# Another order of all engines' work in a fused windowed attention and highway layer

## The chip, the cores and the metric

The kernel runs on one core of a Trainium2 chip. The metric is the time of one execution on the device in microseconds (us), lower is better. Runs of the same kernel are compared by their median.

## The reference

Eight batches, eight heads, 576 positions, 64 values per head. Attention looks back over a window of 128 positions and has a bias that falls with the distance (slope by head). Its result, 4608 rows of 512 values, goes through a highway layer.

```python
scores = scale * q @ k.T                                # per batch and head
scores = where((rel >= 0) & (rel < 128), scores - slope[h] * rel, -1e9)
attn = softmax(scores)
x = (attn @ v)  -> rows of 512 (8 heads x 64)           # 4608 x 512
H = maximum(x @ w_h, 0)
T = 1 / (1 + exp(-(x @ w_t + b_t)))
out = T * H + (1 - T) * x
```

## The kernel before

The output is worked on in 36 blocks of 128 rows. A batch has four full blocks (0 to 3) and half a block, and the two halves of two neighbouring batches make one block 4, which carries the number of the odd batch. Keys are taken in five chunks of 128 for each batch (the fifth, with u = 4, is done with the fourth chunk's scores).

Nothing is scheduled by the compiler. The string `ORDER` holds some 650 words; a loop at the end goes through them, and each word issues one small piece of work. Each engine carries out its own instructions in the order of the words, and waits with semaphores where data or a buffer isn't ready. So the order of the words is the order of every queue: TensorE (PE), VectorE (DVE), ScalarE (ACT), GpSimd (POOL), and SyncE (SP), which only starts transfers. A word is a letter and its indices (batch, then block or chunk).

| word | what it issues | engine, line |
|---|---|---|
| `q b` (and `Q` at the start for halves of batch 0) | loads q and then k of a batch, turned to bf16 on the way | GpSimd's queue, L117 (L120) |
| `V b u`, `v b u` | loads a chunk of v, f32 | SyncE's queue; ScalarE's queue (L126) |
| `L i` | loads w_h or w_t | GpSimd's queue, L134 |
| `h` | one tiny write that keeps the load of V02 from starting early | VectorE, L139 |
| `T b w h` | transposes q (w=0) or k (w=1) of four heads | VectorE, L208 |
| `C b u`, `c b u` | casts a chunk of v to bf16 | GpSimd; ScalarE (L130) |
| `S b u` | scores of a chunk with its mask, into the one tile `sc` | TensorE, L229 and L246 |
| `E b u` | exp of `sc` | ScalarE, L260 |
| `P b t` | probabilities times v for a block, into the one tile `av` | TensorE, L289 |
| `N b t` | reciprocal of the sums and x | VectorE, L299 and L300 |
| `U b t` | transposes x | TensorE, L307 |
| `X b t`, `x b t` | copies the transposed x out | ScalarE; VectorE (L312) |
| `B b t` then `Z b t` | bias into the one tile `z`, then x @ w_t | ScalarE, L317, then TensorE, L332 |
| `z b t` | the same with the bias by a matmul | TensorE, L321 and L332 |
| `Y b t` | tanh of `z` | ScalarE, L338 |
| `H b t` | x @ w_h into the one tile `h` | TensorE, L344 |
| `R b t` | relu(h) - x | VectorE, L349 |
| `o b t`, `O b t` | tanh to gate | GpSimd; VectorE (L353) |
| `G b t`, `g b t` | times gate | GpSimd; VectorE (L357) |
| `A b t`, `a b t` | plus x, gives the output tile `ot` | GpSimd; VectorE (L361) |
| `D b t` | stores the block | SyncE's queue, L368 (L372 for block 4) |
| `M b` | clears the half-filled chunk of a v buffer | GpSimd, L204 |
| `i`, `J`, `F`, `f`, `k` | constants, masks and the bias | several |

A few buffers tie the words together: q and k have three loaded sets (batch b and b + 3 share one) and two transposed sets, v has three loaded and four cast sets, exp has four tiles and one more, `x` ten, and `tt`, `uu` and `ot` six each. `sc`, `av`, `z` and `h` have one.

Of the kernel before, what the change touches and what calls it, by code (L numbers as in the profile page):

```python
# [11 lines left out]


ORDER = """
i2 J V00 Q000 V01 i0 Q010 i1 Q001 Q011 q1 c00 i4 c01 M2 F L1 v03 L0 T000 T010 M1 q2 T001 f h
T011 k V02 V10 i5 V04 S00 E00  S01 P00 E01 N00 T101 U00 S02 X00 P01 E02 z00 N01 T111 U01 S03 x01
V14 c02 T100 Y00 V11 P02 E03 o00 H00 T110 z01 R00 N02 H01 Y01 c03 g00 o01 U02 a00 S10 X02 R01
P03 E10 G01 z02 N03 H02 A01 Y02 B03 U03 O02 R02 S11 X03 V12 C10 T210 G02 P10 E11 Z03 V23 N10 A02
H03 V21 Y03 U10 C11 R03 S12 X10 O03 V13 C12 B10 T211 P11 E12 G03 H10 V20 N11 Z10 A03 T201 V22
U11 Y10 q3 S13 x11 R10 D01 c13 P12 E13 O10 z11 C23 N12 D00 C14 V30 g10 U12 T200 H11 A10 X12 D02  # L20
Y11 D03 P13 R11 c04 C21 D10 S20 c22 N13 o11 B12 H12 g11 c20 A11 E20 U13 Z12 x13 R12 P14 H13 Y12
N14 B13 o12 S21 R13 q4 g12 U14 Z13 x14 a12 P20 Y13 H14 D12 N20 E21 D11 z14 O13 T300 G13 U20 X20
S22 R14 A13 Y14 T311 P21 E22 z20 D13 N21 V34 H20 O14 Y20 T301 U21 o20 S23 X21 T310 P22 E23 z21
N22 V24 C30 g14 U22 V31 R20 A14 S30 X22 T411 Y21 P23 E30 G20 z22 N23 A20 H21 T410 Y22 V32 U23
o21 R21 S31 X23 V33 B23 g21 P30 E31 H22 N30 V40 C31 Z23 a21 R22 U30 V41 C32 Y23 S32 x30 q5 B30
O22 P31 g22 V44 E32 O23 Z30 N31 A22 D14 H23 T401 V42 Y30 C40 U31 D21 S33 X31 R23 D22 B31 T400
V43 G23 P32 c34 H30 E33 N32 A23 Z31 o30 U32 c33 S40 x32 Y31 R30 P33 B32 g30 H31 E40 N33 A30 Z32
O31 R31 U33 c24 G31 S41 x33 Y32 P34 E41 A31 z33 N34 q6 T501 H32 Y33 D20 D23 B34 U34 T510 V54 S42
o32 X34 V50 o33 P40 E42 R32 Z34 C41 V51 N40 G32 H33 T511 Y34 U40 A32 S43 X40 R33 B40 P41 T500
E43 G33 H34 N41 Z40 A33 c42 U41 Y40 o34 S50 x41 R34 o40 P42 E50 g34 H40 N42 A34 z41 R40 c43 g40  # L30
U42 Y41 A40 S51 x42 V52 T610 P43 E51 C54 z42 N43 D32 C50 o41 T611 H41 Y42 V53 B43 U43 o42 T601
S52 X43 C44 D33 D31 P50 C51 E52 R41 Z43 D30 q7 N50 D34 H42 g41 Y43 T600 U50 S53 X50 o43 R42 C53
P51 E53 A41 z50 N51 g42 C52 D41 U51 Y50 H43 V62 x51 B51 a42 o50 D40 P52 V60 R43 Z51 g43 N52 A43
S60 Y51 U52 H50 X52 E60 P53 R50 z52 N53 H51 g50 Y52 O51 A50 B53 U53 R51 S61 x53 G51 T701 H52 E61
V61 P54 A51 V63 R52 Z53 O52 c62 N54 V71 C60 S62 Y53 T700 B54 o53 U54 H53 X54 D42 C61 g52 E62 P60
A52 R53 Z54 D51 N60 H54 V64 G53 Y54 D52 T711 U60 D43 o54 S63 X60 D50 R54 c63 A53 V72 P61 T710
B60 V73 H60 E63 G54 N61 Z60 A54 R60 U61 Y60 S70 x61 V70 O60 P62 g60 E70 A60 z61 V74 N62 C72 U62
D54 H61 X62 Y61 P63 R61 B62 o61 S71 N63 c64 C70 Z62 E71 g61 A61 U63 H62 x63 c71 D61 P70 Y62 S72
D53 N70 D60 B63 o62 U70 E72 Z63 x70 R62 P71 G62 H63 Y63 N71 B70 S73 o63 R63 c73 A62 g63 U71 Z70
x71 a63 C74 P72 Y70 H70 N72 B71 o70 E73 Z71 R70 U72 G70 H71 x72 Y71 P74 A70 R71 z72 N74 o71 D70  # L40
D63 U74 g71 H72 X74 a71 Y72 P73 D71 R72 o72 z74 D62 N73 G72 Y74 U73 H74 x73 o74 z73 A72 R74 g74
H73 Y73 a74 o73 D74 R73 D72 g73 a73 D73
"""


# [384 lines left out]
```

## Time and profile before

| what | value |
|---|---|
| time, median of 3 runs | 155.78 us (155.69 to 158.38) |
| the profiled execution's own time | 155.89 us |
| span of the profiled execution | 154.1 us, mean granted TensorE clock 0.995 |
| busy: TensorE, VectorE, ScalarE, GpSimd | 128.7, 121.3, 111.4, 93.0 us |
| moved by transfers | 29.76 MB, mean 193 GB/s |

The span goes from the first to the last instruction, and the time is a little longer. The profile's slices cut the span into 40 equal parts and show the busy share of each engine in tenths. The chain of work that ended last is followed back from the last instruction, at each step to what released it. A matmul's own duration overlaps that of the next, so the chain's pieces, and not the durations, add up. Line numbers are those of the code above.

### The profile page before, as it was taken

What the parts mean: (1) busy time and instruction counts of PE and PEld (TensorE: products, weight loads), DVE (VectorE), ACT (ScalarE), POOL (GpSimd) and SP (SyncE); (2) the same over time, 40 slices, a digit from 0 to 9 for tenths busy, and PEclk for the clock granted to TensorE, in tenths of its full rate; (3) what the DMA queues carried; (4) which work ended last, traced back from release to release, by engine and by line L of the source; (5) the groups of instructions that cost most, each with busy time, mean ns of one, the idle gap of its engine ahead of it and who ended that gap; (6) DMA issues with size and microseconds to landing.
All of it is one profiled execution on the core that took longest, in us unless ns stands there. A gap on an engine that the chain in (4) does not pass through costs nothing.

```text
span 154.1 us, 6258 instructions
## 1 busy us (share of the span) xinstructions
PE 128.7 (83%) x2754; PEld 73.0 (47%) x2754; DVE 121.3 (79%) x234; ACT 111.4 (72%) x127; POOL 93.0 (60%) x117
## 2 busy tenths in 40 slices
PE   0005489999999999999999996999999999999940
PEld 0001256455655565456665654554555656555510
DVE  5795158979997997799779975999699966796790
ACT  2222675899898698699999987685779989964410
POOL 7940001279985544865679987584297966577640
PEclk9999999999999999999999999999999999999997
DMA  4999999999999999999998999379993891500715
GB/s 107 197 206 207 202 201 209 212 174 207 273 156 200 311 242 271 202 200 188 213 284 194 207 235 327 120 116 192 303 239 120 260 218 41 208 5 3 269 37 167
DMA packets 48222, 29.76 MB, mean 193 GB/s; under 512 B 38466, under 2 KB 39490, under 8 KB 48196
## 3 DMA queue, kind: packets, MB, share of 16 engines
q1 hardware_dynamic: 41712, 18.62, 48.5%
q0 software_dynamic: 5440, 10.49, 38.4%
q10 hardware_dynamic: 1044, 0.27, 1.0%
q8 instruction: 21, 0.34, 0.9%
q14 instruction: 5, 0.04, 0.1%
HBM read 30.41 MB, written 9.44 MB: 259 GB/s over the span
## 4 chain that ended last, share of the span: by engine, by line
PE 47%; DVE 27%; DMA 8%; POOL 5%; issue 5%; ACT 4%; POOLq 0%; DVEq 0%
PE h L344 11%; PE z L332 11%; PE av L289 8%; DMA ld<-in_k_dram 8%; DVE tr L208 7%; PE sc L229 7%; DVE x L300 5%; DVE uu L349 4%; PE av L307 4%; PE sc L246 4%; DVE ot L361 3%; DVE uu L357 2%; ACT pr L260 2%; POOL ot L361 1%; POOL uu L357 1%
## 5 line engine op out<-in xcount | busy, mean ns | idle before, releaser
L260 ACT ACTIVATE pr<-sc 128x2048 bf16<-128x2048 f32 x28 | 52.6, 1877 | 7.6 <-PE sc L246 7.5
L361 POOL TENSOR_TENSOR ot<-uu,x 128x512 f32<-128x512 bf16 x28 | 32.3, 1155 | 13.9 <-DVE uu L357 13.0
L208 DVE STREAM_TRANSPOSE tr<-ld 128x576 uint32<-128x576 uint32 x32 | 38.9, 1242 | 1.7 <-DMA ld<-in_k_dram 1.7
L332 PE MATMUL z<-wT,xt 128*128 128x512 bf16 x144 | 37.8, 386 | 0.0
L344 PE MATMUL h<-wH,xt 128*128 128x512 bf16 x144 | 37.0, 379 | 0.1
L353 POOL TENSOR_SCALAR tt<-tt 128x512 f16<-128x512 f16 x25 | 15.6, 628 | 30.7 <-ACT tt L338 30.7
L338 ACT ACTIVATE tt<-z 128x512 f16<-128x512 f32 x36 | 21.5, 597 | 10.7 <-PE z L332 10.7
L349 DVE SCALAR_TENSOR_TENSOR uu<-h,x 128x512 bf16<-128x512 f32 x36 | 24.5, 682 | 4.2 <-PE h L344 4.2
L300 DVE TENSOR_TENSOR x<-av,rd 128x512 bf16<-128x512 f32 x36 | 24.9, 691 | 1.4
L289 PE MATMUL av<-va,pr 128*128 128x65 bf16 (+1 forms) x480 | 22.2, 197 | 0.4 <-DVE xt L312 0.3
L229 PE MATMUL sc<-tr,tr 32*64 32x192 bf16 (+2 forms) x1152 | 20.2, 253 | 2.8 <-ACT pr L260 2.0
L229 PEld LDWEIGHTS <-tr 32*64 32x64 bf16 x1152 | 13.4, 108 | 18.7 <-issue 15.5
L357 POOL TENSOR_TENSOR uu<-uu,tt 128x512 bf16<-128x512 bf16 x15 | 17.3, 1156 | 7.9 <-DVE uu L349 6.1
L289 PEld LDWEIGHTS <-pr 128*128 128x128 bf16 (+1 forms) x480 | 18.6, 101 | 6.8 <-issue 2.3
L332 PEld LDWEIGHTS <-xt 128*128 128x128 bf16 x144 | 13.5, 99 | 13.4 <-issue 1.0
L344 PEld LDWEIGHTS <-xt 128*128 128x128 bf16 x144 | 12.8, 98 | 12.2 <-issue 0.6
L307 PE MATMUL av<-ident,x 128*128 128x128 bf16 x144 | 14.5, 225 | 2.2 <-DVE x L300 2.0
L299 DVE RECIPROCAL rd<-av 128x8 f32<-128x8 f32 x36 | 7.0, 193 | 11.9 <-PE av L289 11.6
L307 PEld LDWEIGHTS <-x 128*128 128x128 bf16 x144 | 10.2, 100 | 12.5 <-DVE x L300 7.2
L312 ACT COPY xt<-av 128x512 bf16<-128x512 bf16 x19 | 11.1, 585 | 5.6 <-PE av L307 5.3
L130 POOL CAST va<-vs 128x512 bf16<-128x512 f32 x22 | 13.7, 632 | 1.5 <-DMA vs<-in_v_dram 1.5
L130 ACT CAST va<-vs 128x512 bf16<-128x512 f32 x18 | 11.0, 618 | 4.7 <-DMA vs<-in_v_dram 4.6
(47 smaller groups left out, 109.4 us busy)
## 6 DMA issues: line engine op xcount, KB each, us to landing
out_dram<-ot SPq DMA_DIRECT2D x32, 256.0 KB, 4.3
vs<-in_v_dram SPq DMA_DIRECT2D x31, 256.0 KB, 5.6
ld<-in_q_dram POOLq DMA_DIRECT2D x7, 576.0 KB, 8.3
ld<-in_k_dram POOLq DMA_DIRECT2D x7, 576.0 KB, 11.9
vs<-in_v_dram SPq DMA_DIRECT2D x8, 128.0 KB, 5.4
out_dram<-ot SPq DMA_DIRECT2D x8, 128.0 KB, 2.9
ld<-in_q_dram POOLq DMA_DIRECT2D x2, 288.0 KB, 6.9
ld<-in_k_dram POOLq DMA_DIRECT2D x2, 288.0 KB, 7.4
```

Source lines behind the costliest of these rows:

```text
L130: (eng.copy if eng is nc.scalar else eng.tensor_copy)(out=VA[b % 4][:, u, :, 0:D], in_=VS[b % 3][:, u])
L208: nc.vector.transpose(out=t[:, 0:S, :].rearrange("p s e -> p (s e)").bitcast(U32).rearrange("p (s t) -> p t s", t=NT), in_=ld[:, h].bitcas ...
L229: nc.tensor.matmul(out=SC[64 * g : 64 * g + 64, j, 256 * h + col : 256 * h + col + n], lhsT=TR[b % 2, 1, h][rows, key : key + 64, e], rhs= ...
L260: nc.scalar.activation(out=p[:].rearrange("p j h n -> p j (h n)"), in_=SC[:], func=ACTF.Exp, scale=scale)
L289: nc.tensor.matmul(out=av[o : o + m, h, 65 * j : 65 * j + 65], lhsT=PT[bb, pt][:, j, h, off : off + m], rhs=VA[bb % 4][:, u, 4 * h + j, :] ...
L300: nc.vector.tensor_tensor(out=x[:].rearrange("p (h j d) -> p h j d", h=2, j=NJ), in0=av[:, :, :, 0:D], in1=rd[:].to_broadcast([P, 2, NJ, D ...
L307: nc.tensor.transpose(out=AV[blk][:, c // 2, 272 + 64 * (c % 2) :][:, 0:64].bitcast(BF16), in_=X[blk][:, c * P : (c + 1) * P], identity=id ...
L332: nc.tensor.matmul(out=pz[:], lhsT=xt[:, c * P : (c + 1) * P], rhs=wT[:, c, :], start=False, stop=c == NC - 1, skip_group_check=True)
L344: nc.tensor.matmul(out=pa[:], lhsT=xt[:, c * P : (c + 1) * P], rhs=wH[:, c, :], start=c == 0, stop=c == NC - 1)
L349: nc.vector.scalar_tensor_tensor(out=uu[:], in0=PA.pop(blk)[:], scalar=0.0, in1=X[blk][:], op0=ALU.max, op1=ALU.subtract)
L357: eng.tensor_tensor(out=UU[blk][:], in0=UU[blk][:], in1=TT.pop(blk)[:], op=ALU.mult)
L361: eng.tensor_tensor(out=ot[:], in0=UU.pop(blk)[:], in1=X.pop(blk)[:], op=ALU.add)
```

## The change

Only the string `ORDER` is replaced. The new order comes from a search over orders, in which transfers were taken to last longer and to land later, and TensorE's instructions to run at a lower rate. No function is changed. The word counts that differ are those where a word has two forms on two engines:

| | B + Z | z | X | x | C | c | O | o | G | g | A | a | V | v |
|---|---|---|---|---|---|---|---|---|---|---|---|---|---|---|
| before | 19 | 17 | 19 | 17 | 22 | 18 | 11 | 25 | 15 | 21 | 28 | 8 | 39 | 1 |
| after | 13 | 23 | 20 | 16 | 20 | 20 | 15 | 21 | 10 | 26 | 27 | 9 | 37 | 3 |

The first lines, a stretch in the middle and the end of both orders:

```diff
-i2 J V00 Q000 V01 i0 Q010 i1 Q001 Q011 q1 c00 i4 c01 M2 F L1 v03 L0 T000 T010 M1 q2 T001 f h
-T011 k V02 V10 i5 V04 S00 E00  S01 P00 E01 N00 T101 U00 S02 X00 P01 E02 z00 N01 T111 U01 S03 x01
-V14 c02 T100 Y00 V11 P02 E03 o00 H00 T110 z01 R00 N02 H01 Y01 c03 g00 o01 U02 a00 S10 X02 R01
-P03 E10 G01 z02 N03 H02 A01 Y02 B03 U03 O02 R02 S11 X03 V12 C10 T210 G02 P10 E11 Z03 V23 N10 A02
...
-N14 B13 o12 S21 R13 q4 g12 U14 Z13 x14 a12 P20 Y13 H14 D12 N20 E21 D11 z14 O13 T300 G13 U20 X20
-S22 R14 A13 Y14 T311 P21 E22 z20 D13 N21 V34 H20 O14 Y20 T301 U21 o20 S23 X21 T310 P22 E23 z21
-N22 V24 C30 g14 U22 V31 R20 A14 S30 X22 T411 Y21 P23 E30 G20 z22 N23 A20 H21 T410 Y22 V32 U23
...
-D63 U74 g71 H72 X74 a71 Y72 P73 D71 R72 o72 z74 D62 N73 G72 Y74 U73 H74 x73 o74 z73 A72 R74 g74
-H73 Y73 a74 o73 D74 R73 D72 g73 a73 D73
+i2 J V00 Q000 V01 V10 i0 Q010 i1 Q001 Q011 M1 q1 i4 c00 V14 L1 L0 T000 T010 T001 c01 V12 h F v02
+f v03 T011 k S00 E00 S01 P00 E01 N00 i5 T100 U00 S02 X00 T110  P01 V11 c10 E02 z00 N01 U01 Y00
+S03 x01 T111 z01 T101 V13 c14 C02 E03 q2 P02 H00 N02 o00 S10 R00 V20 c03 U02 Y01 H01 x02 E10 O01
+V22 g00 P03 R01 A00 z02 g01 N03 A01 H02 Y02 c11 U03 C12 S11 x03 R02 P10 E11 O02 z03 N10 G02 U10
+A02 X10 S12 Y03 H03 v04 o03 E12 P11 R03 z10 N11 V21 C13 H10 T210 M2 q3 U11 R10 S13 X11 V30 Y10
...
+R11 U13 q4 S20 X13 O11 g11 Y12 P14 a11 E20 z13 N14 U14 Y13 x14 S21 O12 P20 E21 H12 N20 z14 R12
...
+P22 R14 V32 Y20 N22 S30 B21 H20 T410 E30 D00 C23 U22 Z21 T400 D01 C33 X22 S31 T411 V31 o20 Y21
+P23 o13 E31 z22 D02 N23 D03 D11 g13 U23 c30 A12 g14 V24 S32 x23 Y22 D10 R20 P30 E32 V34 A13 z23
...
+o22 S33 X31 V43 R22 C34 c24 P32 o23 g22 E33 a22 Z31 V42 q5 N32 H23 O30 Y31 q6 U32 S40 x32 D12
+c41 O31 R23 P33 E40 H30 N33 D13 V50 R30 U33 S41 X33 c40 P34 c43 H31 N34 E41 z32 R31 g30 U34 Y32
+H32 x34 g23 P40 R32 z33 N40 S42 Y33 U40 z34 X40 T510 P41 Y34 H33 E42 N41 o34 z40 T511 D20 V44
...
+N60 Z54 R52 U60 g52 Y54 S62 T700 X60 H53 E62 D41 C61 O54 T710 V74 A51 P61 V63 z60 N61 A52 R53
+S63 Y60 D50 C62 T701 D42 U61 G53 H54 D52 X61 D43 T711 B61 P62 V70 A53 E63 Z61 R54 N62 G54 H60
...
+E73 O70 g70 U72 a70 H71 x72 D70 Y71 P74 D63 R71 o71 z72 D61 N74 g71 U74 Y72 H72 A71 x74 B74 P73
+R72 D71 Z74 N73 D62 Y74 O72 U73 H74 B73 x73 o74 g72 Z73 A72 R74 g74 H73 Y73 a74 D72 o73 R73 D74
+g73 a73 D73
```

More of the change, by code (lines that the diff above doesn't have):

```diff
@@ L14 @@
 ORDER = """
-i2 J V00 Q000 V01 i0 Q010 i1 Q001 Q011 q1 c00 i4 c01 M2 F L1 v03 L0 T000 T010 M1 q2 T001 f h
-T011 k V02 V10 i5 V04 S00 E00  S01 P00 E01 N00 T101 U00 S02 X00 P01 E02 z00 N01 T111 U01 S03 x01
-V14 c02 T100 Y00 V11 P02 E03 o00 H00 T110 z01 R00 N02 H01 Y01 c03 g00 o01 U02 a00 S10 X02 R01
-P03 E10 G01 z02 N03 H02 A01 Y02 B03 U03 O02 R02 S11 X03 V12 C10 T210 G02 P10 E11 Z03 V23 N10 A02
-H03 V21 Y03 U10 C11 R03 S12 X10 O03 V13 C12 B10 T211 P11 E12 G03 H10 V20 N11 Z10 A03 T201 V22
-U11 Y10 q3 S13 x11 R10 D01 c13 P12 E13 O10 z11 C23 N12 D00 C14 V30 g10 U12 T200 H11 A10 X12 D02
@@ L21 @@
-Y11 D03 P13 R11 c04 C21 D10 S20 c22 N13 o11 B12 H12 g11 c20 A11 E20 U13 Z12 x13 R12 P14 H13 Y12
-N14 B13 o12 S21 R13 q4 g12 U14 Z13 x14 a12 P20 Y13 H14 D12 N20 E21 D11 z14 O13 T300 G13 U20 X20
-S22 R14 A13 Y14 T311 P21 E22 z20 D13 N21 V34 H20 O14 Y20 T301 U21 o20 S23 X21 T310 P22 E23 z21
-N22 V24 C30 g14 U22 V31 R20 A14 S30 X22 T411 Y21 P23 E30 G20 z22 N23 A20 H21 T410 Y22 V32 U23
-o21 R21 S31 X23 V33 B23 g21 P30 E31 H22 N30 V40 C31 Z23 a21 R22 U30 V41 C32 Y23 S32 x30 q5 B30
-O22 P31 g22 V44 E32 O23 Z30 N31 A22 D14 H23 T401 V42 Y30 C40 U31 D21 S33 X31 R23 D22 B31 T400
@@ L27 @@
[L27 to L38, printed above, removed]
@@ L39 @@
-D53 N70 D60 B63 o62 U70 E72 Z63 x70 R62 P71 G62 H63 Y63 N71 B70 S73 o63 R63 c73 A62 g63 U71 Z70
-x71 a63 C74 P72 Y70 H70 N72 B71 o70 E73 Z71 R70 U72 G70 H71 x72 Y71 P74 A70 R71 z72 N74 o71 D70
-D63 U74 g71 H72 X74 a71 Y72 P73 D71 R72 o72 z74 D62 N73 G72 Y74 U73 H74 x73 o74 z73 A72 R74 g74
-H73 Y73 a74 o73 D74 R73 D72 g73 a73 D73
+i2 J V00 Q000 V01 V10 i0 Q010 i1 Q001 Q011 M1 q1 i4 c00 V14 L1 L0 T000 T010 T001 c01 V12 h F v02
+f v03 T011 k S00 E00 S01 P00 E01 N00 i5 T100 U00 S02 X00 T110  P01 V11 c10 E02 z00 N01 U01 Y00
@@ new lines @@
+S03 x01 T111 z01 T101 V13 c14 C02 E03 q2 P02 H00 N02 o00 S10 R00 V20 c03 U02 Y01 H01 x02 E10 O01
+V22 g00 P03 R01 A00 z02 g01 N03 A01 H02 Y02 c11 U03 C12 S11 x03 R02 P10 E11 O02 z03 N10 G02 U10
+A02 X10 S12 Y03 H03 v04 o03 E12 P11 R03 z10 N11 V21 C13 H10 T210 M2 q3 U11 R10 S13 X11 V30 Y10
+T200 G03 P12 E13 z11 N12 V23 A03 T211 U12 c04 H11 o10 X12 T201 G10 Y11 P13 V33 c20 z12 N13 A10
+R11 U13 q4 S20 X13 O11 g11 Y12 P14 a11 E20 z13 N14 U14 Y13 x14 S21 O12 P20 E21 H12 N20 z14 R12
+c21 T301 G12 U20 Y14 S22 X20 T300 o14 E22 P21 C22 H13 T310 z20 N21 R13 S23 T311 U21 E23 H14 x21
@@ new lines @@
+P22 R14 V32 Y20 N22 S30 B21 H20 T410 E30 D00 C23 U22 Z21 T400 D01 C33 X22 S31 T411 V31 o20 Y21
+P23 o13 E31 z22 D02 N23 D03 D11 g13 U23 c30 A12 g14 V24 S32 x23 Y22 D10 R20 P30 E32 V34 A13 z23
+N30 T401 U30 V40 C31 H21 X30 A14 Y23 O21 P31 R21 z30 C32 g20 N31 A20 H22 V41 Y30 g21 B31 a21 U31
+o22 S33 X31 V43 R22 C34 c24 P32 o23 g22 E33 a22 Z31 V42 q5 N32 H23 O30 Y31 q6 U32 S40 x32 D12
+c41 O31 R23 P33 E40 H30 N33 D13 V50 R30 U33 S41 X33 c40 P34 c43 H31 N34 E41 z32 R31 g30 U34 Y32
+H32 x34 g23 P40 R32 z33 N40 S42 Y33 U40 z34 X40 T510 P41 Y34 H33 E42 N41 o34 z40 T511 D20 V44
@@ new lines @@
+U41 c42 D14 R33 S43 X41 D21 T500 Y40 P42 E43 V51 A23 H34 N42 z41 o40 T501 o33 U42 A30 O32 S50
+X42 g32 R34 Y41 P43 E50 g31 o41 z42 g33 G34 N43 D22 H40 T610 c50 D23 A32 Y42 U43 V54 S51 R40 X43
+V52 T611 A31 P50 E51 H41 N50 A33 z43 R41 D32 C51 U50 D31 Y43 g40 S52 A34 x50 D30 B50 a40 V53 P51
+E52 Z50 G41 N51 H42 T601 o43 V60 Y50 o42 U51 c52 S53 R42 q7 X51 T600 B51 P52 E53 H43 D33 A41 N52
+Z51 g42 V61 R43 c53 A42 U52 S60 X52 g43 Y51 D34 A43 P53 D40 c60 z52 V62 N53 C44 O51 C54 U53 Y52
+O50 H50 x53 B53 P54 E60 R50 Z53 N54 G50 H51 Y53 U54 a50 o53 S61 X54 R51 o52 B54 P60 E61 H52 G51
@@ new lines @@
+N60 Z54 R52 U60 g52 Y54 S62 T700 X60 H53 E62 D41 C61 O54 T710 V74 A51 P61 V63 z60 N61 A52 R53
+S63 Y60 D50 C62 T701 D42 U61 G53 H54 D52 X61 D43 T711 B61 P62 V70 A53 E63 Z61 R54 N62 G54 H60
+V64 Y61 D51 U62 R60 C63 S70 V71 X62 O60 A54 B62 O61 P63 g60 E70 H61 N63 A60 Z62 R61 U63 D54 C70
+Y62 S71 x63 D60 g61 B63 o62 V72 P70 a61 E71 H62 N70 Z63 R62 D53 C71 V73 U70 g62 Y63 S72 x70 A62
+B70 P71 E72 H63 o63 N71 Z70 R63 C72 U71 g63 Y70 H70 x71 A63 c64 P72 B71 R70 C73 S73 N72 C74 Z71
+E73 O70 g70 U72 a70 H71 x72 D70 Y71 P74 D63 R71 o71 z72 D61 N74 g71 U74 Y72 H72 A71 x74 B74 P73
```

## Prediction

> **What bounds the kernel now.** I read the busy times first, then the slices, then the chain that ended last.
>
> ```profile
> PE 128.7 (83%) x2754; PEld 73.0 (47%) x2754; DVE 121.3 (79%) x234; ACT 111.4 (72%) x127; POOL 93.0 (60%) x117
> ...
> PE   0005489999999999999999996999999999999940
> ...
> DMA  4999999999999999999998999379993891500715
> ...
> PE 47%; DVE 27%; DMA 8%; POOL 5%; issue 5%; ACT 4%; POOLq 0%; DVEq 0%
> ```
>
> Four engines are within 36 us of each other, so no single total says what the order is worth. The slices say more: a slice is 3.85 us, TensorE is empty for three of them, works from there to the last two with one visible dip, and the transfers are at 9 for the first 22 slices. The chain has 47% TensorE. To see how full TensorE really is I price one block by the chain's view, where a row ends when the next work can start (start, length, work):
>
> ```profile
> 82.71 0.48 PE sc L229 x31
> 83.19 0.31 PE sc L246 x16
> 83.51 0.43 PE av L289 x8
> 83.94 0.86 PE z L332 x4
> 84.80 0.86 PE h L344 x4
> 85.67 0.22 PE av L307 x4
> ...
> 86.81 0.62 PE av L289 x16
> ...
> 91.78 0.22 PE z L321
> ```
>
> So scores (S) are 0.79, P is 0.43 for a batch's first block and 0.62 to 0.64 else, U 0.22, H 0.86, and Z 0.86, which is 1.08 as z, with its bias matmul. For a batch's fourth scores I take 0.91. Added up along the words of the old order these make 121.2 us in all. I now set the sum of all TensorE words up to a block's P against the start of that block's x on VectorE:
>
> ```profile
> 31.76 0.69 DVE L300 TENSOR_TENSOR x<-av,rd 128x512 bf16<-128x512 f32 x1
> ...
> 59.41 0.69 DVE L300 TENSOR_TENSOR x<-av,rd 128x512 bf16<-128x512 f32 x1
> ...
> 62.72 1.26 DVE L208 STREAM_TRANSPOSE tr<-ld 128x576 uint32<-128x576 uint32 x1 [1.69 <-DMA ld<-in_k_dram]
> ...
> 64.04 0.69 DVE L300 TENSOR_TENSOR x<-av,rd 128x512 bf16<-128x512 f32 x1
> ...
> 96.46 0.69 DVE L300 TENSOR_TENSOR x<-av,rd 128x512 bf16<-128x512 f32 x1
> ...
> 107.49 0.69 DVE L300 TENSOR_TENSOR x<-av,rd 128x512 bf16<-128x512 f32 x1
> ...
> 144.19 0.69 DVE L300 TENSOR_TENSOR x<-av,rd 128x512 bf16<-128x512 f32 x1
> ```
>
> The x rows are blocks 03, 22, 23, 43, 52 and the last, 73. The sums up to them are 11.0, 37.8, 40.6, 71.4, 81.0 and 117.1, so the lag of the clock behind the sum is 20.8, 21.6, 23.4, 25.1, 26.5 and 27.1 us. Where the lag stands still, TensorE works without a hole. It grows by 6.3 us after block 03, in steps: 1.8 at block 23 (k of batch 4 lands late, the 1.69 in the row above), 1.7 by block 43, 1.4 by block 52 and 1.4 in small pieces. The step at 43 is this row of the chain, time with no cause that the profile shows:
>
> ```profile
> 94.11 1.52 issue
> ```
>
> So the kernel is TensorE from 13.8 us on, plus 6.3 us of waits, plus a tail of 154.1 − 144.2 = 9.9 us. The profiled execution took 155.89 us, 1.8 over its span, and 0.1 above the median of 155.78; I sum against 155.9.
>
> **The change part by part.** Counting words: S, E, P, N, U, Y, H, R, T, D are as many as before.
>
> *Bias.* Six copies of the bias on ScalarE (B, 19 to 13) become bias matmuls (z, 17 to 23). At 0.22 each TensorE gets **+1.3 us**, 121.2 to 122.5; nothing hides it, since TensorE is the bound, so its ends are 0 (if they fall into waits) and 1.3.
>
> *VectorE, GpSimd, ScalarE.* These are the groups (busy, mean ns), then the spread of the gate's product (minimum, median, maximum in ns), then the first and the last of the six stretches that I summed (length, busy of PE, PEld, DVE, ACT, POOL):
>
> ```profile
> L361 POOL TENSOR_TENSOR ot<-uu,x 128x512 f32<-128x512 bf16 x28 | 32.3, 1155 | 13.9 <-DVE uu L357 13.0
> ...
> L353 DVE TENSOR_SCALAR tt<-tt 128x512 f16<-128x512 f16 x11 | 5.1, 465 | 1.0 <-ACT tt L338 0.9
> ...
> L357 DVE TENSOR_TENSOR uu<-uu,tt 128x512 bf16<-128x512 bf16 x21 | 10.6, 506 | 1.2 <-POOL tt L353 0.3
> ...
> L361 DVE TENSOR_TENSOR ot<-uu,x 128x512 f32<-128x512 bf16 x8 | 6.3, 788 | 0.1
> ...
> L357 DVE TENSOR_TENSOR uu<-uu,tt x21: 412/425/1178, 29.4 to 149.1; 128x512 bf16<-128x512 bf16 x21
> ...
> 30.00:48.00 18.00, 17.75 (x414) 10.27 (x414) 16.13 (x28) 16.74 (x21) 15.11 (x18) 1.00 1.10 205
> ...
> 114.00:130.00 16.00, 15.99 (x364) 9.24 (x363) 13.72 (x26) 14.95 (x18) 12.96 (x15) 1.00 0.68 183
> ```
>
> VectorE gets 4 more O (4 × 465), 5 more g (5 × 506), one more a (788) and one x less (about 0.4): +4.8 us, 121.3 to 126.1. GpSimd loses 5 G and one A (1155 each), 4 o and 2 C (a bit over half of that each): −10.7. ScalarE loses six B, gains one X and two c, and issues two more V loads. I price all this at 0: VectorE stands idle for 14.5 us between 30 and 130 us (100 minus its busy time in the six stretches, 85.5), which covers 4.8. Without that cover it is the second rival. The Trainium skill's page "SBUF — State Buffer", section "Who interferes with whom", says that a VectorE instruction with two SBUF inputs contends with a GpSimd instruction that reads SBUF. The trace agrees that something of the kind is there (L357 on VectorE takes 412 at least, 425 in the middle, 1178 at most); by the rule fewer GpSimd instructions would take some of the 81 ns between mean and median away, under 2 us of VectorE in all, and the time stays.
>
> *The scores' single buffer.* S writes the one tile `sc`, so TensorE's work between two S must cover the exp:
>
> ```profile
> 41.31 0.69 PE L289 MATMUL av<-va,pr 128*128 128x65 bf16 x16
> 41.54 1.88 ACT L260 ACTIVATE pr<-sc 128x2048 bf16<-128x2048 f32 x1 [0.15 <-PE sc L246]
> ```
>
> The exp starts 0.23 after TensorE has issued its last score, takes 1.88, and the next S can follow 0.05 later: 2.16 us. In the old order one S after the start has less work ahead of it (S30, 1.94). In the new one S12 has 1.73 (P10, z03, U10), S30 and S41 1.72, and S21, S31, S32 1.94. The shortfalls that are new add up to 0.43 + 0.22 + 0.44 + 3 × 0.22 = 1.75. A wait that another delay covers costs nothing, so the ends are 0 and 1.75; I take the middle, **+0.9**.
>
> *The loads.* (Group of transfers: how many, KB each, us from issue to landing; the first is the load between 48 and 66 us, the next two those between 66 and 90.)
>
> ```profile
> ld<-in_k_dram POOLq DMA_DIRECT2D x1, 576.0 KB, 12.2
> ...
> vs<-in_v_dram SPq DMA_DIRECT2D x6, 256.0 KB, 8.3
> ...
> ld<-in_k_dram POOLq DMA_DIRECT2D x2, 576.0 KB, 10.7
> ```
>
> In the old order q4 (line L117) stands 10.9 us of TensorE's work ahead of T411, its first use of k; in the new one 13.8 ahead of T410. Its k took 12.2 us to land, so **−1.7** of the step at block 23. But q5 shrinks from 13.1 to 11.6 ahead of T510. k is issued 0.75 after q; landing 10.7 to 12.2 later makes 11.45 to 12.95, so VectorE waits 0 to 1.35 for it. I take **+0.3**. Stores wait: D00 moves from 22 us of TensorE's sum to 40, behind the loads. An ot buffer is written again six blocks later; the shortest distance from store to that write is 2.8 against 2.7 before, so 0.
>
> *The start.* `h` holds SyncE until VectorE has passed three transposes; old order: only V00 and V01 are ahead of it. New: V10, V14 and V12 too (0.64 MB), while the first q and k come in until 11.75. The rows are the cast that waited for V01, the last k half (issued at 3.45), T011, and the queues' packets, MB and share from 14 to 30 us:
>
> ```profile
> 7.73 0.62 ACT L130 CAST va<-vs 128x512 bf16<-128x512 f32 x1 [2.93 <-DMA vs<-in_v_dram]
> ...
> ld<-in_k_dram POOLq DMA_DIRECT2D x1, 288.0 KB, 8.3
> ...
> 12.51 1.26 DVE L208 STREAM_TRANSPOSE tr<-ld 128x576 uint32<-128x576 uint32 x1
> ...
> q0 software_dynamic: 1776, 2.62, 89.9%
> q1 hardware_dynamic: 1589, 0.40, 19.0%
> ```
>
> The V queue had 0.40 of 3.3 MB, 12%. From 7.7, where V01 has landed, to 11.75 (3.45 + 8.3) that is 0.5 us later for the k half that T011 needs 0.8 after: **+0.5** with the halves before it late as well, ends 0 and the whole 0.64 MB at 205 GB/s (3.28 MB in 16 us), 3.1.
>
> *Steps at 43 and 52.* These waits (1.7 and 1.4) belong to where the old order happens to put things; a new order has its own. I take half of them as gone: **−1.5**, ends 0 and −3.1.
>
> *Tail.*
>
> ```profile
> 146.23 0.69 DVE L349 SCALAR_TENSOR_TENSOR uu<-h,x 128x512 bf16<-128x512 f32 x1 [0.37 <-PE h L344]
> ```
>
> From the last x on both orders run U73, x73, Z73, H73, R73, g73, a73, D73; the new one has O72 and g72 (0.97) on VectorE in it, before R74 (the row, which waits 0.37 for h as it is), and no bias matmul (0.22): 0.
>
> Sum: 155.9 + 1.3 + 0.9 − 1.7 + 0.3 + 0.5 − 1.5 = **155.7 us**.
>
> **The rivals.**
> 1. *TensorE's waits go altogether.* For it: the order is planned on longer transfers, and the chain's DMA share is 8%. All 6.3 us gone, with the bias and the start: 155.9 − 6.3 + 1.3 + 0.5 = 151.4. Against: the new score waits.
> 2. *VectorE becomes the bound* (the slow side). If its idle time between 30 and 130 us is where it waits for TensorE in a fixed order, 4.8 us more work moves every N by as much: 155.9 + 4.8 = 160.7. It decides where VectorE shows no idle time any more ahead of a block's reciprocal:
>
> ```profile
> DVE rd L299 <- PE av L289: 11.6, 9, 5.0
> ...
> POOL va L130 <- DMA vs<-in_v_dram: 1.5, 2, 1.0
> ```
>
> That is 11.6 us now, 5.0 of it at one block. For it: 79% busy already. Against: TensorE's 83%, and the x rows above, which follow TensorE's sum.
> 3. *A V load behind the late stores.* D00 to D11 go out within 4.6 us of TensorE's work, V31 in their midst with 4.5 to its cast C31 and 1.5 more to P31; V70 likewise behind four stores, and c41 sits on ScalarE ahead of an exp, 4.5 after V41. V loads between 66 and 90 us took 8.3 to land, so each can be up to 2 to 3 late: 155.7 + 3 = 158.7. Against: the smallest such distance before was 3.2, past the start, and GpSimd's casts waited 1.5 in all (second row above).
> 4. *The early V loads cost the start their full 3.1* instead of 0.5: 158.3. The Trainium skill's "DMA: Bandwidth & Descriptors", section "Queues, rings and completion order", has each DMA engine go round the queues packet by packet; with packets of one size that would be this case. The rows agree in count (1776 and 1589) and not in bytes (1475 and 252 each), which is for 0.5.
> 5. *The order isn't what it says.* Leads are longer for q4, and the shortest V lead goes from 3.2 to 4.5, but q5's and q3's are shorter; then the load wait only moves: 157.4, within the forecast's own range.
>
> **How the numbers follow.** Chances: forecast with the fifth rival 0.50 (153.5 to 157.9), first rival 0.22, VectorE 0.12, late V loads 0.11, start 0.05. 2%, about what a measurement of this kernel can tell from no change, is 152.7 to 158.9. Faster is the first rival, 0.22; slower is VectorE and a quarter of the late loads, 0.15; the rest, 0.63, is within. The range runs from 151.4, all waits gone, to 159.5, the late loads with another score wait; beyond lie VectorE's case and less than a tenth below.
>
> **What would show it.** Right: the lag at block 03 at 21.3, no step of a DMA at batch 4, TensorE's sum 122.5, "PE sc" waiting for "ACT pr" some 0.2 to 0.4 us at S12, S30 and S41, GpSimd at 82 us, VectorE at 126. Wrong: a lag that grows steadily (VectorE bound), a wait of POOL or ACT "va" for DMA in the middle, a first score after 14.5 us, or a lag that ends near 22.

## The result and the profile after

The new order takes **169.33 us** in the median of four runs (167.92 to 171.00), the old one 155.75 beside it. The ratio, **1.077** (95% interval 1.070 to 1.083), compares the fast runs alone, 167.92 and 167.97 against 155.69 to 155.78, while the profile below is of a slower one, 170.70 (1.8 over its span of 168.9), so up to 2.8 us of what it shows beyond the old one's 155.89 belong to the run and not to the order. The forecast was 155.7, its range ended at 159.5.

The page of the new kernel: busy times, slices (4.2 us each), granted clock, transfers.

```profile
PE 132.6 (79%) x2760; PEld 74.0 (44%) x2760; DVE 128.4 (76%) x243; ACT 109.2 (65%) x124; POOL 84.1 (50%) x105
...
PE   0004589999720999999989998997999989999950
...
PEclk9999999999996599999999999999999999999999
DMA  5999999999999978211379998139999492831514
```

In the old kernel TensorE's row had one small dip. Here slices 11 to 13 read 7, 2, 0: TensorE stands still, and the granted clock of slices 13 and 14 is 0.6 and 0.5. The list of waits (engine, line, what it waited for, us in total, times, longest) says on whom:

```profile
POOL va L130 <- DMA vs<-in_v_dram: 19.1, 1, 19.1
...
ACT va L130 <- DMA vs<-in_v_dram: 9.9, 2, 7.0
...
PE av L289 <- ACT xt L312: 7.6, 2, 7.4
...
ACT pr L260 <- DMA vs<-in_v_dram: 2.5, 1, 2.5
```

GpSimd's 19.1 is one early cast with nothing urgent behind it. ScalarE's 7.0 at a cast and its 2.5 at an exp are new. An exp (L260) that "waits for the load of v" is odd, since it reads no v. The timeline (start, length, what; in brackets the idle time before and its releaser) shows the load `v04` in front of it:

```profile
41.04 0.80 POOL L117 DMA_DIRECT2D ld<-in_q_dram  x1
41.10 0.69 ACTq L126 DMA_DIRECT2D vs<-in_v_dram  x1
41.89 1.88 ACT L260 ACTIVATE pr<-sc 128x2048 bf16<-128x2048 f32 x1 [2.51 <-DMA vs<-in_v_dram]
...
53.93 0.62 ACT L130 CAST va<-vs 128x512 bf16<-128x512 f32 x1 [7.04 <-DMA vs<-in_v_dram]
54.46 0.58 ACT L312 COPY xt<-av 128x512 bf16<-128x512 bf16 x1
...
55.09 1.06 PE L289 MATMUL av<-va,pr 128*128 128x65 bf16 x16 [7.38 <-ACT xt L312]
...
56.37 1.91 PE L332 MATMUL z<-wT,xt 128*128 128x512 bf16 x4
```

Read from below: P13 waited 7.38 us for the copy X12 to free `av`; X12 stood on ScalarE behind the cast c04; c04 waited 7.04 for v04, which was issued at 41.10, just behind q3 on GpSimd's queue (41.04). The group of that transfer (KB, us from issue to landing) with the other two loads of ScalarE's queue:

```profile
vs<-in_v_dram ACTq DMA_DIRECT2D x2, 256.0 KB, 14.0
vs<-in_v_dram ACTq DMA_DIRECT2D x1, 128.0 KB, 12.8
```

Behind the hole the four z matmuls take 1.91 us where they take 1.03 at full clock. A table of stretches (length; busy of PE, PEld, DVE, ACT, POOL; granted clock, DMA share, GB/s) prices the clock:

```profile
47.50:55.00 7.50, 0.21 (x1) 0.00 (x0) 1.14 (x2) 1.07 (x3) 2.00 (x3) 0.80 1.12 247
55.00:60.00 5.00, 4.91 (x103) 3.01 (x105) 2.81 (x6) 2.29 (x6) 0.00 (x0) 0.61 1.03 228
60.00:64.00 4.00, 4.00 (x85) 2.13 (x78) 2.56 (x7) 3.41 (x3) 0.00 (x0) 1.00 0.88 257
```

The Trainium skill's "TensorE: Matmul & The Clock Gate", Part 1, has the clock halved after an idle window of about 3.4 us and back after about as much work; the trace agrees, with 0.61 over the 5 us behind the hole and 1.00 from 60.

Now the prediction's lag (start of a block's x minus TensorE's sum of words up to its P). These x rows are blocks 03, 12, 13, 14 and 73:

```profile
34.42 0.69 DVE L300 TENSOR_TENSOR x<-av,rd 128x512 bf16<-128x512 f32 x1
...
45.70 0.69 DVE L300 TENSOR_TENSOR x<-av,rd 128x512 bf16<-128x512 f32 x1
...
56.43 0.69 DVE L300 TENSOR_TENSOR x<-av,rd 128x512 bf16<-128x512 f32 x1
...
60.52 0.69 DVE L300 TENSOR_TENSOR x<-av,rd 128x512 bf16<-128x512 f32 x1
...
159.00 0.69 DVE L300 TENSOR_TENSOR x<-av,rd 128x512 bf16<-128x512 f32 x1
```

The sums are 11.0, 21.6, 24.4, 27.2 and 118.8, so the lag is 23.5, 24.1, 32.0, 33.3 and 40.2, where the old order had 20.8, 21.3, 21.5, 21.4 and 27.1. The tail behind the last x is 9.9 as before. So the 14.8 us between the two profiled executions are 1.8 more TensorE words ahead of block 73 and 13.1 more lag: 2.8 up to block 12 (2.7 of them by block 03, before `v04` goes out), then 7.7 in one step at block 13, 1.4 at block 14 (the clock), and 1.2 in all the rest.

### The profile page after: what moved, and what is told of

Read it like the earlier page. It is cut to its first block, busy times and chain, and to the rows that moved or that the text cites. A ratio compares the mean times of both kernels' runs of the same rounds, so it can differ in the third digit from the quotient of the medians.

```text
span 168.9 us, 6262 instructions
## 1 busy us (share of the span) xinstructions
PE 132.6 (79%) x2760; PEld 74.0 (44%) x2760; DVE 128.4 (76%) x243; ACT 109.2 (65%) x124; POOL 84.1 (50%) x105
## 5 line engine op out<-in xcount | busy, mean ns | idle before, releaser
L260 ACT ACTIVATE pr<-sc 128x2048 bf16<-128x2048 f32 x28 | 52.5, 1877 | 10.3 <-PE sc L246 7.6
L332 PE MATMUL z<-wT,xt 128*128 128x512 bf16 x144 | 38.7, 393 | 0.6 <-DMA wT<-in_moe_w_t_dram 0.6
L361 POOL TENSOR_TENSOR ot<-uu,x 128x512 f32<-128x512 bf16 x27 | 31.3, 1163 | 14.7 <-DVE uu L357 14.4
L338 ACT ACTIVATE tt<-z 128x512 f16<-128x512 f32 x36 | 21.6, 601 | 14.5 <-PE z L332 14.2
L353 POOL TENSOR_SCALAR tt<-tt 128x512 f16<-128x512 f16 x21 | 13.8, 662 | 24.8 <-ACT tt L338 24.8
L289 PEld LDWEIGHTS <-pr 128*128 128x128 bf16 (+1 forms) x480 | 19.1, 102 | 15.3 <-ACT xt L312 8.4
L299 DVE RECIPROCAL rd<-av 128x8 f32<-128x8 f32 x36 | 7.2, 199 | 22.3 <-PE av L289 21.8
L130 POOL CAST va<-vs 128x512 bf16<-128x512 f32 x20 | 13.1, 664 | 19.1 <-DMA vs<-in_v_dram 19.1
L357 POOL TENSOR_TENSOR uu<-uu,tt 128x512 bf16<-128x512 bf16 x10 | 11.9, 1190 | 19.3 <-DVE uu L349 18.4
L130 ACT CAST va<-vs 128x512 bf16<-128x512 f32 x20 | 12.3, 619 | 9.9 <-DMA vs<-in_v_dram 9.9
L307 PE MATMUL av<-ident,x 128*128 128x128 bf16 x144 | 14.8, 228 | 2.2 <-DVE ident L200 1.2
L312 ACT COPY xt<-av 128x512 bf16<-128x512 bf16 x20 | 11.7, 586 | 7.3 <-PE av L307 6.2
```

Of the source, the lines that this page charges most:

```text
L130: (eng.copy if eng is nc.scalar else eng.tensor_copy)(out=VA[b % 4][:, u, :, 0:D], in_=VS[b % 3][:, u])
L260: nc.scalar.activation(out=p[:].rearrange("p j h n -> p j (h n)"), in_=SC[:], func=ACTF.Exp, scale=scale)
L289: nc.tensor.matmul(out=av[o : o + m, h, 65 * j : 65 * j + 65], lhsT=PT[bb, pt][:, j, h, off : off + m], rhs=VA[bb % 4][:, u, 4 * h + j, :] ...
L307: nc.tensor.transpose(out=AV[blk][:, c // 2, 272 + 64 * (c % 2) :][:, 0:64].bitcast(BF16), in_=X[blk][:, c * P : (c + 1) * P], identity=id ...
L332: nc.tensor.matmul(out=pz[:], lhsT=xt[:, c * P : (c + 1) * P], rhs=wT[:, c, :], start=False, stop=c == NC - 1, skip_group_check=True)
L338: nc.scalar.activation(out=tt[:], in_=PZ.pop(blk)[:], func=ACTF.Tanh, scale=0.5)
```

## The experiments

Times are medians of all runs; ratios, taken as above and with their 95% interval, are to the old order run beside it. "Early V04" is the first kernel below, the base of several others.

**v04 taken off ScalarE.** Early V04:

```diff
-z01 T101 V13 c14 C02 ... S12 Y03 H03 v04 o03
+z01 T101 V13 V04 c14 C02 ... S12 Y03 H03 o03
```

> The new order with one word changed: the half chunk v04, which ScalarE's queue starts 5.7 us of TensorE's work ahead of its cast c04, is started on SyncE's queue right after V13, some 15 us earlier. Theory A (v04 lands late, c04 holds ScalarE for 7 us, TensorE waits 7.4 us and then runs at half clock for a while): the 7.0 us wait of the cast and TensorE's 7.4 us hole are gone, time 158.0 to 160 against 168 to 171. Rival B (VectorE bounds the new order): a wait on ScalarE is only moved, time above 165. Rival C (loads behind the late stores): no change before 60 us matters, above 165.

160.54 us, ratio 1.028 (1.012 to 1.045). The waits at c04 and at the exp are gone, and the x rows show what that is worth (blocks 12, 13, 14, 73):

```profile
43.63 0.69 DVE L299 TENSOR_TENSOR x<-av,rd 128x512 bf16<-128x512 f32 x1
...
46.84 0.69 DVE L299 TENSOR_TENSOR x<-av,rd 128x512 bf16<-128x512 f32 x1
...
49.82 0.69 DVE L299 TENSOR_TENSOR x<-av,rd 128x512 bf16<-128x512 f32 x1
...
148.47 0.69 DVE L299 TENSOR_TENSOR x<-av,rd 128x512 bf16<-128x512 f32 x1
```

Lags 22.0, 22.4, 22.7 and 29.6, no step. The two spans differ by 10.5 us (168.9 to 158.4). Not all of it is the load's: at block 03 the new order's profile is 1.2 us of lag ahead already (23.5 against 22.3), 6.7 us before `v04` goes out, and TensorE had waited 0.56 us for w_t, which landed 1.3 us later than in early V04. By the ratios, 1.077 and 1.028, this single 128 KB load is worth about 7.6 us.

**Queue or moment?** The same place in the words, on SyncE's queue (`-v04 +V04`):

> The new order with v04 started at the same place of the order, but from SyncE's queue (behind V21) instead of ScalarE's. Theory A1 (what is late is the half chunk itself: any queue of v gets a small share while q3 and q4 are loading, and behind V21 it is no sooner): time within 3 us of the new order. Rival A2 (ScalarE's queue is what is slow, or issuing there is what holds ScalarE): v04 lands within 6 us and the time is 158 to 160.

160.70 us, ratio 1.034 (1.024 to 1.043): as with the early one. SyncE holds nothing but transfers and runs ahead of the words, so V04 went out well ahead of q3. The queue's share is not what was tested, the moment is.

**c04 later on ScalarE** (from ahead of H11 to ahead of P14):

> The new order with the load v04 as it is, but its cast c04 moved from before X12 to just before P14, the first work that needs it, about 3.5 us of TensorE's work later. Theory A with ScalarE's strict order as the carrier: X12, Y11, c20, E20 no longer wait behind the cast, so TensorE goes on through P13 and waits only at P14: the wait shrinks from 7.4 to 2 to 5 us, time 162 to 167. If instead the wait is the load's alone and not the queue behind the cast, the time stays at 168 to 171.

165.26, ratio 1.060 (1.049 to 1.071): the late landing costs less when less stands behind its cast, but v04 still lands after 11.6 and E12 is held 3.4.

**v04 earlier, but still on ScalarE** (right behind c11):

> The new order with v04 still on ScalarE's queue, but right after c11, about 4 us of TensorE's work earlier, when no load of q or k is on its way, so that it has landed or nearly so when q3 starts. Theory A (v04 shares the transfer engines with q3, and q4 after it, and gets 12% of the bytes): it lands within 7 us, c04 does not wait, time 158.5 to 161, like v04 on SyncE's queue. Rival A2 (ScalarE's queue itself is slow or blocks ScalarE): 164 or more.

167.47, ratio 1.079 (1.068 to 1.089). Expected was 158.5 to 161; nothing was won. The timeline says why:

```profile
39.77 0.69 ACTq L126 DMA_DIRECT2D vs<-in_v_dram  x1
40.56 1.88 ACT L260 ACTIVATE pr<-sc 128x2048 bf16<-128x2048 f32 x1 [6.34 <-DMA vs<-in_v_dram]
```

v04 lands 4.8 us after its issue and c04 doesn't wait, but the issue itself stood 6.3 us on ScalarE with an exp behind it. In the compiled program, as the trace's records of these transfers show, all that SyncE and ScalarE start take eight completion semaphores in turn, and each is issued only when the transfer before it on the same semaphore has landed. Here that one landed at 39.75 and `v04` went out at 39.77; in the new order itself it was 41.08 and 41.10. On SyncE such a wait holds only other transfers; on ScalarE it stops every exp and copy behind it. The 2.5 us ahead of the exp in the new order are the same thing.

**v04 on ScalarE with an unused semaphore**, among the first loads (right behind c01):

> The new order with v04 left on ScalarE's queue, but issued among the first loads, right behind c01, ahead of any exp, on a completion semaphore that no earlier transfer has used. Theory A (the 9 us are the held ScalarE: a load that waits at its issue or lands late at its cast; the queue as such costs nothing): as with V04 early on SyncE's queue, 158.8 to 161, and ScalarE waits for no V load in the middle. Rival Q (a load of ScalarE's queue is slow or blocks as such): c04 or the first exp waits, 163 or more. At the start the 0.128 MB more could cost up to 0.6.

161.80, ratio 1.037 (1.032 to 1.042). ScalarE waits for no load in the middle. The lag of block 00 is 1.3 above that of early V04 and still is at block 14 (1.8 at the end, 31.4 against 29.6): the start pays for the extra load. So the queue as such is not the cause.

**q3 later, v04 untouched** (q3 from ahead of U11 to behind A03):

> The new order with one word moved: q3, the load of q and k of batch 3, goes on GpSimd's queue behind A03 instead of ahead of G03, about 3.5 us later than it was (41.04). v04 stays on ScalarE's queue where it is. Theory L (v04's 12.8 us to land come of q3, issued 0.06 us ahead of it): v04 lands in 4 to 6 us, c04's wait of 7.0 us goes, the 2.5 us at v04's issue stay: 160.5 to 163. Rival (the landing is slow for another reason, say all the transfers under way or ScalarE's queue): c04 waits as long as before, 167 to 169.

```profile
41.05 0.69 ACTq L126 DMA_DIRECT2D vs<-in_v_dram  x1
41.84 1.88 ACT L260 ACTIVATE pr<-sc 128x2048 bf16<-128x2048 f32 x1 [3.48 <-PE h L344]
42.50 0.80 POOL L117 DMA_DIRECT2D ld<-in_q_dram  x1
...
46.74 0.61 ACT L130 CAST va<-vs 128x512 bf16<-128x512 f32 x1
```

```profile
vs<-in_v_dram ACTq DMA_DIRECT2D x1, 128.0 KB, 4.5
```

163.81, ratio 1.052 (1.039 to 1.065), a little above the range. v04 goes out at the same time as in the new order (41.05), now 1.45 us ahead of q3, lands in 4.5 instead of 12.8, and c04 starts without a wait. So the landing was q3's doing, and that is shown by moving q3 alone. The wait of v04's issue remains (the exp's gap, here put down to TensorE).

**The same load in the old order**: ahead of E12, and right ahead of q3.

> The old order with V04 taken from SyncE's queue near the start and put on ScalarE's queue just before E12, 5.7 us of TensorE's work ahead of c04, as in the new order. Theory A: c04 waits for DMA some 5 to 9 us, the exp behind it too, TensorE's clock falls for a while: 160 to 166 against 155.8. Rivals B and C (the rest of the new order makes it slow): within 1 us of 155.8.

> The old order with V04 moved to ScalarE's queue right beside q3 (after Y10), 4.4 us of TensorE's work ahead of c04, where the earlier try (b_v04_late) put it 2.65 us ahead of q3 and cost nothing. Theory A: it lands 9 to 13 us later, c04 holds ScalarE for 4 to 8 us with the exps behind it, time 160 to 165. If lateness beside q3 is not the cause: within 1.5 us of the old order.

155.01 (0.994, 0.989 to 0.999) and 155.47 (0.999, 0.994 to 1.005); both expectations missed. v04 was issued at 38.04 and 39.48, with hardly a hold (the exp behind it waited 0.51 us in the first and nothing in the second) and ahead of q3 (40.69 and 39.87); the second landed in 4.2. A load on ScalarE's queue beside q3 does no harm as such: it took a busy semaphore and a place behind q3. Three of the ten runs of the second did take 161.7 to 163.7, within the expectation; they have no trace, so what they waited for isn't known.

**The other terms**, each put back in early V04. First six z to B + Z; then V10, V14 and V12 behind `h` with i5 ahead of S00; then six scores one TensorE word later (S12, S21, S30, S31, S32, S41); then 44 words of gates, products and sums back on the old order's engines.

> The new order with V04 on SyncE's queue early (a_v04_sync_early), and six blocks' bias (23, 30, 32, 34, 40, 43) put back from a matmul to a copy on ScalarE, each copy right after the tanh that frees the tile. Theory D (TensorE's added work is on the path): 1.3 us faster than a_v04_sync_early. Rival: the matmuls fell into waits that stay, or ScalarE's copies are now late: within 0.5 us or slower.

> The new order with V04 early on SyncE's queue, and the start put back: V10, V14 and V12 behind the hold, and the identity (i5) ahead of the first scores. Theory E (the early v loads take bytes from the first q and k and from w_t): the second half of the first scores starts at 13.8 to 13.9 instead of 14.4 us, z00 no longer waits 0.56 for w_t, time 0.5 to 1.5 us under a_v04_sync_early. Rival: the start is made up for later, within 0.3 us; or the later v loads make new waits, slower.

> The new order with V04 on SyncE's queue right after V13, and with six scores (S12, S21, S30, S31, S32, S41) each moved behind the next word of TensorE, so that at least 2.16 us of TensorE's work stands between two scores of these. Theory S (the single score tile costs the shortfalls added up in the prediction): up to 1.75 us less, 157.5 to 159.5, and the waits of TensorE's scores for ScalarE's exp at these places go. Theory O (TensorE's lag comes of other waits, which then take the same time): within 0.7 us of the 160.2 that V04 alone gave.

> The new order with V04 on SyncE's queue right after V13, and with every gate, product and final sum (o, g, a against O, G, A) back on the engine that it has in the old order: 44 words change engine, 4 O, 5 g and one a leave VectorE on balance. V04 alone gave 158.8 to 160.9 on its undisturbed runs. Theory P (VectorE is what the rest of the loss is: 4.8 us more work, and longer instructions beside it): 1.5 to 3 us less, 156 to 159, and the waits of TensorE for VectorE's x fall from 9.7 to near the old order's 7.2. Theory O (the rest is in the order of the words on TensorE, not in the engines' shares): within 1 us of 160, or slower, since the words were placed for the other engines.

161.80 (1.041, 1.028 to 1.054), 161.03 (1.036, 1.024 to 1.048), 163.29 (1.050, 1.045 to 1.055) and 160.90 (1.034, 1.029 to 1.038), against 1.028 (1.012 to 1.045) for early V04. None gave anything back that these intervals (0.7 to 2.6 us either way) can show; the scores moved later made it worse. Two things blur this. In the second kernel the loads didn't move: V10, V14 and V12 go out at 1.85, 4.56 and 5.35, within 0.01 us of the new order, and the second half of the first scores starts at 14.43 as there. In the new order the load behind `h` is v02 on ScalarE's queue, so `h` doesn't hold SyncE, and theory E was not tested. And in the profiles of the first, second and fourth TensorE stalls for 1.76, 1.21 and 1.34 us inside S23, where early V04 does not (such stalls are the subject of the last section); a gain of about 1 us can hide behind that.

**The two halves joined** at P43: early V04 and then the old order, and the reverse.

> Two halves put together: the new order with V04 on SyncE's queue right behind V13 up to its word P43, and then the words that are left, in the old order. Asked: where the 3 to 5 us lie that the new order still costs once V04 is early. By the lag of block 43 (27.2 against 25.1) and TensorE's sums they grow all along. Theory H1 (the loss is in the first half, where it was read as small waits of about 2 us and the start): 157.5 to 159, most of it still there. Theory H2 (the loss is in the second half, where SyncE's late stores and the V loads lie): 155 to 156.5.

> The counterpart: the old order up to its word P43, then the words that are left, in the new order. Theory H1 (loss in the first half): 155 to 156.5. Theory H2 (loss in the second half): 157.5 to 159.5. If the two theories share it, both halves come out between 156.5 and 158.5; if neither half costs (the loss comes of what the halves do to each other, such as stores put off from the first to the second), both stay within 1 us of the old order.

164.93 (1.064, 1.054 to 1.074) and 159.21 (1.029, 1.021 to 1.036). The second fits a loss in the new second half: its lag is within 0.7 of the old one's up to block 43 and 30.4 at the end, with steps of 2.0 at block 53 (1.65 of it a stall of TensorE, see the last section) and 1.6 at 61 and 62. The first is worse than either parent, with steps of 3.7 at block 23 (1.42 of it such a stall) and 4.3 at 43 that neither parent has. So joining makes waits of its own and the halves locate nothing.

**x ahead of VectorE's other work.** In early V04 the reciprocals of ten blocks start 0.5 to 1.3 us after their P has ended, behind other VectorE words, 8.9 us in all. One word at each goes behind the reciprocal:

```diff
-P21 C22 H13 T310 z20 N21 R13
+P21 C22 H13 z20 N21 T310 R13
```

> The new order with V04 early on SyncE's queue, and with ten words of VectorE (four transposes, four products, two sums or gates: g01, T310, a22, g33, T611, T600, T710, T711, g60, a61) moved from ahead of a block's reciprocal to behind it. In the kernel with V04 alone the reciprocal of these ten blocks starts 0.5 to 1.3 us after its probabilities times v have ended, 8.9 us in all, and TensorE's lag grows at seven of them, 6 us in all. Theory N (what the new order still costs is VectorE's queue: other work stands ahead of the reciprocal and x, and the single tile av holds TensorE): the lag of block 73 falls from 29.6 to 26 to 28, time 157 to 159 against 160.2. Rival O (the same VectorE work then makes the next thing late, a relu that frees h or a transpose that a score needs): 159.5 to 162.

162.61, ratio 1.040 (1.033 to 1.047). Eight of the ten lateness gaps went below 0.3, and the time did not follow. One reason is a stall of 1.91 us in S23 with a granted clock of 0.66 after it (see the last section): 4.1 of lag at block 23. Without that step the lag grows by 6.4 from block 14 to 73, and early V04's, likewise without its step there, by 6.5: the waits came back elsewhere, as the rival said.

**Versions of the old order.** q4 right behind P13; the same with v04 ahead of E12; the same as the first with T110, g43, O52 and T710 behind the reciprocals of 02, 52, 54 and 61.

> The old order, with only q4 moved up to right behind P13, about 5 us of TensorE's work earlier. The prediction's term for the loads: VectorE waits 1.69 us for k of batch 4 at block 23 in the old order, and with the lead longer than the 12.2 us of the load that wait goes: 1.7 less, 153.5 to 154.5. Rival: the load that goes earlier meets the V loads of its time, one of them lands late in turn (as v04 beside q3 does in the new order), or the step comes back later: 155.3 to 157.

> The old order with the two single moves together that each came out ahead of it: q4 right behind P13 (0.993) and V04 as v04 on ScalarE ahead of E12 (0.994). If the two add up: ratio 0.987, about 154. If the second was only the spread of the runs, as no wait in its trace speaks for it: as q4 alone, 0.993, 154.5 to 155.

> The old order with q4 right behind P13, and with T110, g43, O52 and T710 moved behind the reciprocals of blocks 02, 52, 54 and 61, which start 1.51, 0.91, 0.71 and 0.56 after their probabilities times v. Theory N: up to 1.5 us less than with q4 alone (154.99), 153 to 154.5, a version ahead of both kernels. Rival O: within 0.5 of q4 alone, or slower.

154.99 (0.993, 0.990 to 0.996), 154.96 (1.001, 0.997 to 1.005) and 155.82 (1.000, 0.995 to 1.004). Only the first has an interval below 1, but the second took the same time and came out 0.8% higher, so its 0.7% is no more than two such comparisons differ by. The third has a stall of 1.40 us at 85.1 that the first lacks. In the first, k of batch 4 no longer keeps the transpose waiting:

```profile
61.75 1.25 DVE L208 STREAM_TRANSPOSE tr<-ld 128x576 uint32<-128x576 uint32 x1
63.44 0.69 DVE L300 TENSOR_TENSOR x<-av,rd 128x512 bf16<-128x512 f32 x1
```

In the old order that transpose carried a wait of 1.69; block 23's step falls from 1.8 to 0.5, and the lag of block 73 from 27.1 to 25.9.

## Why the prediction was wrong

**The step that failed** is in the part on VectorE, GpSimd and ScalarE: "ScalarE loses six B, gains one X and two c, and issues two more V loads. I price all this at 0." For v04 that 0 was about 7.6 us by the ratios. In the profiles it was 9.4: against early V04, and past the 1.2 at block 03, the lag grows by 0.9 more up to block 12 (the exp held behind the issue), 7.5 more at block 13 (c04) and 1.0 at block 14 (the clock). Three things could have been asked of the old trace and the two orders. The only V load on ScalarE's queue there has this row in the listing of transfers:

```profile
vs<-in_v_dram ACTq DMA_DIRECT2D x1, 256.0 KB, 14.3
```

Against 14.3, the 5.7 us of TensorE's work from v04 to c04 were never worked out, though the third rival did that sum for V31 and V70. The order in which v04 and q3 reach their queues was not asked for, only q4's and q5's leads were. And a transfer was counted as free on an engine that computes, without what stands behind it. The list of signs did name it, "a wait of POOL or ACT 'va' for DMA in the middle"; it had no price.

**What held.** The second half of the first scores, the one that needs T011, starts at 14.43 instead of 13.82, +0.6 where +0.5 was forecast:

```profile
14.43 0.55 PE L229 MATMUL sc<-tr,tr 32*64 32x192 bf16 x16 [0.23 <-DVE tr L208]
```

The direction held: the last q and k halves land 0.7 and 0.9 us later. That the size came so close is partly luck. In the new order `h` does not hold SyncE, so V11 goes out early as well (at 6.92, 0.9 MB in all instead of 0.64), and the wait, 0.39, is one transpose earlier, for a q half. The sign set for block 03, a lag of 21.3, wasn't met: it is 23.5, and 22.3 in early V04. The wait for batch 4's k is gone from block 23, as forecast (in the old order with q4 earlier that took 1.2 off the last lag, where −1.7 was taken). GpSimd's 84.1 and VectorE's 128.4 are near the forecast 82 and 126. VectorE's product of the gate did not get shorter beside fewer GpSimd instructions: its mean went from 506 to 578 ns.

**What was sized wrong besides.** With V04 early the rest comes to about 160.2, which is 4.5 above the forecast and past the end of its range, so v04 alone isn't the whole miss. At block 14 the lag is 1.3 above the old one's, where the start's +0.5 was forecast. From block 14 to block 73 the lag was forecast to grow by 5.7 − 1.7 + 0.3 − 1.5 + 0.9 = 3.7; it grew by 6.9 (22.7 to 29.6), which is 3.2 of the 4.5. TensorE's words ahead of block 73 are 1.8 more and not 1.3, since others moved with the bias matmuls. The −1.5 for steps that the new order would not have was wrong in sign: it has its own at blocks 21, 32, 42 and 43, 51, 61 and 62, 5.8 in all, less small steps back. The score waits, +0.9, come to some 0.6 at S12 and S23 of early V04; giving the scores more room made it slower.

**The rivals.** The third, a late V load ahead of an exp on ScalarE, is what happened, but at c04 and behind a load of q and k, not behind stores, and at 7.6 us where it had 3. VectorE as the bound had 160.7, near what is left without v04, and that is no support for it: putting 44 words back on the old engines or putting x first gained nothing. Its queue is late at single blocks; that this sets the end is not shown. What makes up those 4.5 us stays open; no single term tried gave them back, and the stalls of the last section blurred several of the tries.

## What to carry to other kernels

A transfer started from a computing engine is two waits in that engine's queue: the issue may wait for an older transfer's completion semaphore, and everything behind the consumer waits for the landing; put it on an engine with nothing else, or early. A small load issued just behind a large one on another queue can take as long as the large one, since the two took turns packet for packet here, so compare the order of issue, and not only the leads. When an order is replaced, sum the distance from every load to its first user, the odd ones first.

## What the runs showed of the hardware

A 128 KB load on ScalarE's queue landed in 4.2 and 4.5 us when issued 0.39 and 1.45 us ahead of a q of 576 KB (and in 4.8 when it was 5.3 us ahead), and in 11.6 and 12.8 when issued 0.98 and 0.06 us behind it. The two queues' packets in the new kernel (packets, MB):

```profile
q0 software_dynamic: 5440, 10.49, 34.7%
q10 hardware_dynamic: 2612, 0.66, 1.9%
```

That is 1928 bytes a packet on GpSimd's queue and 252 on ScalarE's. In the new order from 44 to 51 us, with q3 and v04 both under way, the two moved packets one for one (SyncE's queue, q1, between them):

```profile
q0 software_dynamic: 439, 0.97, 76.2%
q1 hardware_dynamic: 277, 0.48, 20.7%
q10 hardware_dynamic: 435, 0.11, 9.4%
```

With q3 later the same queue moved 495 packets in the one microsecond from 42.5 to 43.5. So v04's 512 small packets took turns with as many large ones, and it paid by the packet and not by the byte. At the 62 packets a microsecond of these rows 512 take 8.3 us, an estimate; with the 2.2 us from the issue to the first packet (43.27) that is most of the 12.8. By bytes at 205 GB/s the same packets would have come to 5.4.

TensorE's stalls "without a cause" have places. The stretches from 0 to a stall (with matmuls and weight loads counted), of the old order ahead of block 43's stall of 1.52 us, and of the kernel with x first ahead of its 1.91:

```profile
0.00:95.60 95.60, 77.25 (x1759) 44.46 (x1760) 76.29 (x153) 72.40 (x80) 57.10 (x75) 1.00 1.08 216
```

```profile
0.00:63.40 63.40, 42.02 (x981) 24.24 (x992) 47.20 (x101) 38.54 (x41) 29.09 (x43) 1.00 1.06 213
```

The weight loads, the second count, were 1760 and 992, both 96 more than a multiple of 128. In the twenty profiles of this case there are 25 such stalls of 0.6 us or more, and all lie at 352, 992, 1504, 1632, 1760 or 2016; each of these is 96 more than a multiple of 128 too. 128 pairs of weight load and matmul are 256 instructions; the page's row for the queue "instruction" fits this:

```profile
q8 instruction: 21, 0.34, 0.8%
```

21 packets of 16 KB are 21 blocks of 256 instructions at 64 bytes, and TensorE's 2760 pairs make 21.6 such blocks. The packets' own times in the traces agree. Let the n-th packet belong to the border at 96 + 128 n (the second to 352, the seventh to 992). TensorE then never started on the pairs behind a border sooner than 1.24 us after its packet had landed (400 borders in twenty profiles), and all 25 stalls ended 1.27 to 1.65 us after it. So in these stalls TensorE waits for the next block of its program. Why a block lands late isn't shown, and no run took a block away. The step at block 43, of which the forecast took half away with the order, then belongs to the count of instructions and to the moment at which a block lands. The stall of 1.91 us cost clock too: the kernel with x first was granted 0.66 from 63.4 to 68.0. That is a shorter pause than the idle window of about 3.4 us in the Trainium skill's "TensorE: Matmul & The Clock Gate", Part 1; the measurement decides, though TensorE had been busy for only 0.54 of the 2.4 us before. The length of the stall alone doesn't decide it: 0.61 was granted behind stalls of 1.21 and 1.42 us (the start put back, the new first half), and 1.00 behind those of 1.76 and 1.52 us (the bias put back, the old order).
